# General path into the Else of one branch, other PSUM tiles for the splits, and POOL's weight residues in quarters: attention and mixture-of-experts kernel on one Trainium2 core

## Chip, cores and metric

The kernel runs on one core of a Trainium2 chip. The metric is the device time of one execution in microseconds (us): before the change a median of 1216.23 over 3 runs (1215.79 to 1216.82). PE is TensorE, DVE VectorE, ACT ScalarE, POOL GpSimd, SP SyncE.

## What is computed

An attention whose score maps are mixed over the 12 heads before and after the softmax, and a mixture of 8 experts on its rows, of which each row goes to one. All is fp32.

```python
B, H, S, D = 8, 12, 448, 64
s = einsum('bhij,hg->bgij', q @ k.T / sqrt(64), w_pre)
p = exp(s - s.max(-1)); p = p / (p.sum(-1) + 1e-9)
x = (einsum('bgij,gh->bhij', p, w_post) @ v)      # laid out as 3584 rows of 768
logits = x @ w_gate                               # 8 experts
e = logits.argmax(1); g = softmax(logits)[e]
out[row] = g * (relu(x[row] @ w1[e]) @ w2[e])     # w1: 768 x 1024, w2: 1024 x 768
```

## The kernel before

**Attention, to some 690 us.** The queries are worked off in tiles (`T`), and each tile in smaller steps: score matmuls (L275), a matmul that mixes heads (L308), reduce and exponentials (L314, L322), the inverse of the sums (`recip`, L330 and L332, operations on 124x2 elements in SBUF), the weights of the second mixing on POOL (L339), its matmuls (L355), and the product with v (L395, L417). The order of all this on every engine is written out by hand. At the end of each tile the rows of x go to DRAM, the expert of each row is chosen on VectorE (`choose`, `mark`), PE counts the rows of each expert by matmuls with the one-hot rows `ohb` (`rank`, L503), and `place` turns the counts into positions. `token`, `number` and `scatter` (L541 to L556) write the token's number and gate into the expert's list `TB` in DRAM.

**Getting expert 0 ready, beside the end of the attention.** A product of fp32 values is made from parts: a rounded value and its residue, three products instead of one. For expert 0's `w1`, six panels of 128x1024, the rounded part is ScalarE's (`round_w`), and the residue (raw less rounded) comes from `rest_w` (L583): panels 0 to 2 on POOL, between its L339 operations, and 3 to 5 on VectorE. The rows of expert 0 come in four slots of 128, gathered by indirect DMA. `turn` (L617) transposes a slot on PE into two PSUM tiles (part 0 is columns 0 to 255 of 768, part 1 the other 512), for slots 2 and 3 with rows of the last tile added by another matmul (L631). `split_x` (L633) rounds a part on ScalarE (L639) and takes the residue on VectorE (L640). Slot 0 uses the two banks of PSUM tile bs_106, slots 1 and 2 those of bs_107, slot 3 the tiles bm_108 and bm_109.

**The branches.** A number `flags` is computed from the counts (L911 to L918): bit e says that expert e has over 384 rows, the bits above the eighth that some expert has over 512. Only in the latter case is `beyond` needed, the general path: a loop over extra slots, each with its own gathers, weights, matmuls and stores. It has PSUM and SBUF pools of its own. Then the experts follow: `hidden(e, n)` is the first layer for n rows (8 x 6 x 3 = 144 matmuls at L1141, into four PSUM tiles pm_h, the first on the bank of bs_106 that slot 0's part 1 had), `result` the second layer for a slot (L1164). `hidden` exists in two copies, for 384 and 512 rows, behind a branch (L1186), and slot 3's `result` behind another (L1197).

With the data of these runs expert 0 has no more than 384 rows, and the general path isn't taken.

```python
with tc.If((flags >> NE) > 0):            # L1039
    beyond()
...
for e in range(NE):
    begin(e)
    long = (flags >> e) & 1
    widths = (CAP, SHORT) if e else (SHORT, CAP)          # 512 and 384
    with tc.If(long > 0 if e else long < 1) as cmp:       # L1186
        hidden(e, widths[0])
    with cmp.Else():
        hidden(e, widths[1])
```

Of the kernel before, what the change touches and what calls it, by code (L numbers as in the profile page):

```python
# [8 lines left out]
F32 = mybir.dt.float32  # L9
# [5 lines left out]
AF = mybir.ActivationFunctionType  # L15
ALU = mybir.AluOpType
AX = mybir.AxisListType
PSUM = bass.MemoryType.PSUM
# [3 lines left out]
HD = H * D  # L22
NT = B * S
NE, FF = 8, 1024
P = 128
# [9 lines left out]
CAP = 512  # L35
# [10 lines left out]
def attn_moe_kernel(ctx, tc, qT, kT, v, w_pre, w_post, w_gate, w1, w2, out):  # L46
# [536 lines left out]
    def rest_w(kt, engine):  # L583
        hi, lo = W["a", 0, kt]
        engine.tensor_sub(out=lo, in0=RAW.pop(("a", 0, kt)), in1=hi.bitcast(F32))
# [78 lines left out]
    side, side2 = ([bank[:, n, :] for n in (1, 0)] for bank in bank_s)  # L664
# [202 lines left out]
    turn(0, side)  # L867
# [9 lines left out]
    turn(1, side2)  # L877
# [7 lines left out]
    split_x(0, side)  # L885
    evict_x(T, 0)
    av(T, (1,), bank_m[1:])
    split_x(1, side2, (0,))
    evict_x(T, 1)
    split_x(1, side2, (1,))  # L890
# [9 lines left out]
    token(T - 1)  # L900
    number(T - 1)
    scatter(T - 1)
    gate(T)
    place(T)
    turn(2, side2, T)
# [18 lines left out]
    split_x(2, side2)  # L924
    rest_w(5, nc.vector)
    turn(3, bank_m, T)
    split_x(3, bank_m)
# [12 lines left out]
    def beyond():  # L940
# [11 lines left out]
        nc.vector.tensor_copy(out=total, in_=cum[:, NE - 1:NE])  # L952
        nslots = nc.values_load(total[0:1, 0:1], min_val=0, max_val=NT // P,
                                skip_runtime_bounds_check_because="a count of tokens over P")
        with tc.For_i(0, nslots, 1):
# [37 lines left out]
            xs = rt([P, HD], "oxs")  # L993
# [4 lines left out]
            u1 = rt([P, NK1, FF], "u1")  # L998
            u2 = rt([P, NK2, HD], "u2")
            for n, (u, w, nk) in enumerate(((u1, w1, NK1), (u2, w2, NK2))):  # L1000
                flat = w.rearrange("e r c -> (e r) c")
                for kt in range(nk):
                    nc.gpsimd.indirect_dma_start(
                        out=u[:, kt, :], out_offset=None, in_=flat,
                        in_offset=bass.IndirectOffsetOnAxis(ap=wi[:, n, kt:kt + 1], axis=0),
                        bounds_check=flat.shape[0] - 1, oob_is_err=False)
            xT = rt([P, NK1, P], "oxT")
            for kt in range(NK1):
                px = rest_ps.tile([P, 512], F32, name="opx")
                nc.tensor.transpose(out=px[:, :P], in_=xs[:, kt * P:(kt + 1) * P], identity=ident)  # L1010
                nc.vector.tensor_copy(out=xT[:, kt, :], in_=px[:, :P])
            hT = rt([P, NK2, P], "ohT")
            for ft in range(NK2):
                ph = rest_ps.tile([P, 512], F32, name="oph")
                for kt in range(NK1):
                    nc.tensor.matmul(out=ph[:, :P], lhsT=u1[:, kt, ft * P:(ft + 1) * P],
                                     rhs=xT[:, kt, :], start=(kt == 0), stop=(kt == NK1 - 1))
                nc.scalar.activation(out=hT[:, ft, :], in_=ph[:, :P], func=AF.Relu)
            yo = rt([P, HD], "oy")
            for g in range(2):  # L1020
                gs = slice(g * 384, (g + 1) * 384)
                py = rest_ps.tile([P, 512], F32, name="opy")
                for kt in range(NK2):
                    nc.tensor.matmul(out=py[:, :384], lhsT=hT[:, kt, :], rhs=u2[:, kt, gs],
                                     start=(kt == 0), stop=(kt == NK2 - 1))
                nc.vector.tensor_scalar(out=yo[:, gs], in0=py[:, :384], scalar1=tb[:, 1:2],
                                        scalar2=None, op0=ALU.mult)
# [4 lines left out]
    with ExitStack() as more:  # L1032
        rest = more.enter_context(tc.tile_pool(name="rest", bufs=1))
        rest_ps = more.enter_context(tc.tile_pool(name="rest_ps", bufs=1, space=PSUM))

        def rt(shape, name, dt=F32):
            return rest.tile(shape, dt, name=name)

        with tc.If((flags >> NE) > 0):  # L1039
            beyond()  # L1040
# [139 lines left out]
    for e in range(NE):  # L1180
        HH[e] = tuple(h_p.tile([P, NK2, CAP], F32R, name=f"h{x}") for x in "hl")
        begin(e)
        asked, order = dict(RAW), list(RAWS)
        long = (flags >> e) & 1
        widths = (CAP, SHORT) if e else (SHORT, CAP)
        with tc.If(long > 0 if e else long < 1) as cmp:  # L1186
            hidden(e, widths[0])
        RAW.clear()
        RAW.update(asked)
        RAWS[:] = order  # L1190
        with cmp.Else():
            hidden(e, widths[1])
# [38 lines left out]
```

## Time and profile before

| | us | share of the span |
|---|---|---|
| median of 3 runs | 1216.23 | |
| the profiled execution | 1215.08 | |
| its span | 1213.4 | |
| PE busy | 1183.0 | 97% |
| weight loads of PE busy | 992.4 | 82% |
| VectorE busy | 798.5 | 66% |
| ScalarE busy | 724.6 | 60% |
| POOL busy | 392.7 | 32% |

The profile is of one execution. Its time is 1.15 us under the median of the runs, and 1.7 us of it lie around the span. [...] Times of rows are in us from the start of the span. A timeline row gives start, duration, engine, line, operation, output and inputs, and in brackets how long the engine stood idle before and what ended that. PEld are the weight loads of PE, and an engine's name with q is its sequencer (branches, semaphores).

### The profile page before, as it was taken

The numbers are of one execution on the slowest core, as the hardware profiler recorded it, in microseconds if no ns is written. First come the engines' busy times: TensorE is split into PE (matmuls) and PEld (weight loads), VectorE is DVE, ScalarE is ACT, GpSimd is POOL, SyncE is SP. The second block draws the span as 40 slices with busy tenths as digits, with TensorE's granted clock in tenths as the row PEclk, the third lists the DMA queues.
The fourth block names the chain that finished last, engine by engine and source line by source line (L and its number), as shares of the span: only waits on it lengthen the run. The fifth ranks groups of instructions, "written<-read, shape, count | busy, mean of one in ns | idle before, by whom it ended". The sixth has DMA issues, their size and how long they took to land. (4 is left out here: it accounts for less than half of the span.)

```text
span 1213.4 us, 46361 instructions
## 1 busy us (share of the span) xinstructions
PE 1183.0 (97%) x19435; PEld 992.4 (82%) x19437; DVE 798.5 (66%) x1988; ACT 724.6 (60%) x1491; POOL 392.7 (32%) x613
## 2 busy tenths in 40 slices
PE   7999999999999999999999999999999999999996
PEld 3677787777777777877777799898989899989886
DVE  5887888878878878888788845444535344544320
ACT  5877777878777868778776545343434344444220
POOL 4443453544534535435344412020202002110100
PEclk9999999999999999999999999999999999999998
DMA  6666657566656566575656487465655647575300
GB/s 190 206 188 190 195 160 219 173 182 201 197 168 204 175 202 197 162 218 188 177 175 191 134 239 223 140 204 159 188 155 148 167 133 218 164 227 131 119 18 34
DMA packets 178793, 211.19 MB, mean 174 GB/s; under 512 B 85573, under 2 KB 156245, under 8 KB 178568
## 3 DMA queue, kind: packets, MB, share of 16 engines
q1 hardware_dynamic: 172504, 184.14, 52.0%
q0 software_dynamic: 6064, 23.86, 5.7%
q8 instruction: 164, 2.69, 1.0%
q14 instruction: 61, 0.50, 0.2%
HBM read 97.59 MB, written 23.07 MB: 99 GB/s over the span
## 5 line engine op out<-in xcount | busy, mean ns | idle before, releaser
L322 ACT ACTIVATE et<-bm,st 124x448 f32<-124x448 f32 x360 | 225.4, 631 | 156.6 <-DVE st L314 130.9
L314 DVE TENSOR_REDUCE st<-bm 124x1 f32<-124x448 f32 x360 | 208.4, 619 | 73.7 <-PE bm L308 67.0
L355 PEld LDWEIGHTS bp<-wp,et 64*64 64x64 f32 (+1 forms) x10052 | 196.5, 135 | 71.2 <-issue 49.1
L1141 PE MATMUL pm_h<-si,ah 128*128 128x512 f32 (+1 forms) x768 | 230.2, 381 | 3.1 <-DVE si L640 2.0
L373 DVE COPY pt<-bp 128x480 f32<-128x480 f32 x350 | 212.1, 648 | 2.4 <-PE bp L355 1.8
L339 POOL TENSOR_SCALAR wp<-Wpost,st 124x60 f32<-124x60 f32 x360 | 151.6, 436 | 170.0 <-DVE st L332 135.4
L355 PE MATMUL bp<-wp,et 64*64 64x60 f32 (+1 forms) x10052 | 190.4, 218 | 1.2 <-issue 1.1
L308 PE MATMUL bm<-sb,Wquad 60*60 60x448 f32 (+3 forms) x1408 | 185.1, 560 | 5.3 <-ACT et L322 3.5
L1141 PEld LDWEIGHTS pm_h<-si,ah 128*128 128x128 f32 x768 | 142.6, 188 | 29.8 <-issue 4.2
L285 ACT COPY si<-bs 120x896 f32<-120x896 f32 (+1 forms) x189 | 161.5, 910 | 3.8 <-PE bs L275 2.1
L1141 PE MATMUL pm_h<-si,al 128*128 128x512 f32 (+1 forms) x384 | 146.1, 380 | 0.0
L1145 DVE SCALAR_TENSOR_TENSOR hl<-pm_h,hh 128x512 fp32r<-128x512 f32 (+1 forms) x64 | 42.1, 658 | 140.8 <-ACT hh L1144 140.8
L417 PE MATMUL bs<-pt,vt 128*64 128x120 f32 (+1 forms) x2400 | 127.4, 261 | 1.2 <-ACT et L322 0.8
L1164 PE MATMUL pm_y<-bh,hl 128*128 128x384 f32 x480 | 121.8, 334 | 0.0
L1164 PE MATMUL pm_y<-bh,hh 128*128 128x384 f32 x480 | 121.8, 334 | 0.0
L1164 PE MATMUL pm_y<-bl,hh 128*128 128x384 f32 x480 | 121.8, 334 | 0.0
L1144 ACT ACTIVATE hh<-pm_h 128x512 fp32r<-128x512 f32 (+1 forms) x64 | 36.5, 571 | 141.3 <-PE pm_h L1141 141.3
L151 POOL TENSOR_TENSOR ql<-qr,qh 128x360 fp32r<-128x360 f32 (+1 forms) x78 | 69.8, 906 | 156.5 <-ACT qh L150 120.8
L656 POOL DMA_INDIRECT si<-XD,tcl x28 | 39.7, 1417 | 247.9 <-DVE y L1169 234.7
L417 PEld LDWEIGHTS bs<-pt,vt 128*64 128x64 f32 x2400 | 114.9, 137 | 5.7 <-issue 1.0
L1173 POOL DMA_INDIRECT out<-y,ti x30 | 31.1, 1038 | 187.4 <-ACT y L1171 71.6
L1164 PEld LDWEIGHTS pm_y<-bh,hh 128*128 128x128 f32 x480 | 86.8, 188 | 0.5
(172 smaller groups left out, 1731.7 us busy)
## 6 DMA issues: line engine op xcount, KB each, us to landing
sb<-si SPq DMA_DIRECT2D x344, 210.0 KB
wraw<-in_w SPq DMA_DIRECT2D x48, 512.0 KB
wraw<-in_w SPq DMA_DIRECT2D x64, 384.0 KB
vt<-in_v SPq DMA_DIRECT2D x64, 192.0 KB
kr<-in_kT SPq DMA_DIRECT2D x42, 224.0 KB
XD<-xr SPq DMA_DIRECT2D x48, 180.0 KB
qr<-in_qT SPq DMA_DIRECT2D x46, 180.0 KB
sb<-si SPq DMA_DIRECT2D x16, 189.0 KB
```

Of the source, the lines that this page charges most:

```text
L151: engine.tensor_sub(out=lo, in0=src, in1=hi.bitcast(F32))
L285: copy(out=SI[T][:ni, 2 * c:2 * c + 2, :], in_=bank[:ni, :, :S])
L308: nc.tensor.matmul(out=bank_m[r][CUT[c], :S], lhsT=Wquad[CUT[r], CUT[c]], rhs=sb[CUT[r], c, :], start=True, stop=True)
L314: nc.vector.reduce_max(out=st[:R1, 0, c:c + 1], in_=bank_m[c][:R1, :S], axis=AX.X, negate=True)
L322: nc.scalar.activation(out=et[:R1, c, :], in_=bank_m[c][:R1, :S], func=AF.Exp, bias=st[:R1, 0, c:c + 1], scale=1.0, accum_out=st[:R1, 1, c ...
L339: nc.gpsimd.tensor_scalar(out=wp[:R1, c, :H * IQ], in0=Wpost[:R1], scalar1=st[:R1, 2, c:c + 1], scalar2=None, op0=ALU.mult)
L355: nc.tensor.matmul(out=banks[r][col * JC:(col + 1) * JC, at_:at_ + W], lhsT=et[CUT[r], n, kg * JC:(kg + 1) * JC], rhs=wp[CUT[r], n, :W], s ...
L373: copy(out=flat[:, :, i0 + r * IB:i0 + (r + 1) * IB] .rearrange("p x (n k) -> p x n k", k=IQ), in_=banks[r][:, :2 * NJ * W].rearrange("p ( ...
L417: nc.tensor.matmul(out=HOME[T, g][r * D:(r + 1) * D, p, :], lhsT=VV[b][:, c, h * D:(h + 1) * D], rhs=PT[T][:, c, h, :ni], start=(c == 0), ...
L1141: nc.tensor.matmul(out=ph[:, :n], lhsT=wx[:, fs], rhs=xx, start=(m == 0), stop=(m == 3 * NK1 - 1))
L1145: nc.vector.scalar_tensor_tensor(out=hl[:, ft, :n], in0=ph[:, :n], scalar=0.0, in1=hh[:, ft, :n].bitcast(F32), op0=ALU.max, op1=ALU.subtract)
L1164: nc.tensor.matmul(out=py[g][:, :384], lhsT=hx[:, kt, ts], rhs=wx[:, g * 384:(g + 1) * 384], start=(n == 0), stop=(n == 3 * NK2 - 1))
```

## The change

There are four parts to it.

1. `rest_w` on POOL goes in four pieces of 256 columns; on VectorE it stays whole.
2. `homes` gives the slots other PSUM tiles: slot 0 bs_106 as before, slot 1 one bank of bs_107 and bp_111, slot 2 the other bank of bs_107 and bm_109, slot 3 bank 0 of bs_106 and bm_108.
3. `token`, `number` and `scatter` of the last but one tile move from behind `evict_r(T, 1)` to between the two parts of slot 0's split.
4. `beyond` is no longer called ahead of the experts. One branch asks whether the general path is not needed and expert 0 is short. If so, it runs the short `hidden` of expert 0; all else is in its Else: the general path (behind a branch of its own, followed by a second fetch of four `w2` panels), and expert 0's short and long `hidden`. The general path uses the experts' storage (hx, tx, RAWS, the pools y and pm_y) and streams the weights in panels.

```diff
     def rest_w(kt, engine):
-        hi, lo = W["a", 0, kt]
-        engine.tensor_sub(out=lo, in0=RAW.pop(("a", 0, kt)), in1=hi.bitcast(F32))
+        raw, (hi, lo) = RAW.pop(("a", 0, kt)), W["a", 0, kt]
+        width = FF // 4 if engine is nc.gpsimd else FF
+        for c in range(0, FF, width):
+            cs = slice(c, c + width)
+            engine.tensor_sub(out=lo[:, cs], in0=raw[:, cs], in1=hi[:, cs].bitcast(F32))
...
-    side, side2 = ([bank[:, n, :] for n in (1, 0)] for bank in bank_s)
+    homes = ([bank_s[0][:, 1, :], bank_s[0][:, 0, :]], [bank_s[1][:, 1, :], bank_p[1]],
+             [bank_s[1][:, 0, :], bank_m[1]], [bank_s[0][:, 0, :], bank_m[0]])
...
-    split_x(0, side)
+    split_x(0, homes[0], (0,))
+    token(T - 1)
+    number(T - 1)
+    scatter(T - 1)
+    split_x(0, homes[0], (1,))
...
     evict_r(T, 1)
-    token(T - 1)
-    number(T - 1)
-    scatter(T - 1)
     gate(T)
     place(T)
-    turn(2, side2, T)
+    turn(2, homes[2], T)
...
-    split_x(2, side2)
+    split_x(2, homes[2])
     rest_w(5, nc.vector)
-    turn(3, bank_m, T)
-    split_x(3, bank_m)
+    turn(3, homes[3], T)
+    split_x(3, homes[3])
...
-        with tc.If((flags >> NE) > 0):
-            beyond()
...
+        if e == 0:
+            with tc.If((flags & (((1 << NE + 4) - (1 << NE)) | 1)) < 1) as usual:
+                hidden(e, SHORT)
+            again()
+            with usual.Else():
+                with tc.If((flags >> NE) > 0):
+                    beyond()
+                    for kt in range(AHEAD_W):
+                        nc.sync.dma_start(out=RAW["b", e, kt], in_=w2[e, kt * P:(kt + 1) * P, :])
+                with tc.If(long < 1) as cmp:
+                    hidden(e, SHORT)
+                again()
+                with cmp.Else():
+                    hidden(e, CAP)
+        else:
+            with tc.If(long > 0) as cmp:
+                hidden(e, CAP)
...
```

What this makes of the order on the engines, at the places that the prediction speaks of:

ScalarE at the end of the attention phase, before: it reads the flags (`many`) and rounds the parts of slots 2 and 3, with what each waits for.

```order
L918 TENSOR_LOAD many [waits DVE_49]
L639 CAST si<-bs_107 128x2x128 [waits PE_49]
L639 CAST si<-bs_107 128x4x128 [waits DVE_49]
L639 CAST si<-bm_108 128x2x128 [waits PE_49]
L639 CAST si<-bm_109 128x4x128 [waits PE_49]
```

And now:

```order
L923 TENSOR_LOAD many [waits DVE_49]
L642 CAST si<-bs_107 128x2x128 [waits PE_49]
L642 CAST si<-bm_109 128x4x128 [waits PE_49]
L642 CAST si<-bs_106 128x2x128 [waits DVE_49,PE_49]
L642 CAST si<-bm_108 128x4x128 [waits PE_49]
```

The second cast of slot 2 waits for PE in the place of VectorE; slot 3's first part is now in bs_106.

PE before, from the end of the general path to expert 0's first matmuls (`ah` and `al` are a panel's two parts, the loop's branches are L955):

```order
L1024 MATMUL opy<-u_14366,ohT 128x384 x16
L955 REGISTER_ALU
L955 COMPARE_AND_BRANCH
L955 UNCONDITIONAL_BRANCH
L1039 UNCONDITIONAL_BRANCH
L1186 REGISTER_ALU
L1186 COMPARE_AND_BRANCH
L1141 MATMUL pm_h<-si,ah_13364 128x384 x2
```

PE now, at the end of the usual case's first layer and the beginning of what is jumped over:

```order
L1201 UNCONDITIONAL_BRANCH
L1205 REGISTER_ALU
L1205 COMPARE_AND_BRANCH
L963 TENSOR_LOAD total
L965 COMPARE_AND_BRANCH
L965 UNCONDITIONAL_BRANCH x2
L1254 BRANCH_PREFETCH_HINT
L1018 MATMUL pm_y<-ident,hx_14304 128x128 x6
```

The general path stood ahead of expert 0's first layer; it stands behind the usual copy of that layer, inside what the jump at L1201 passes over.

## Rows read from the trace of the kernel before

**Rows 1.** Stretches: window, length, busy of PE PEld DVE ACT POOL, clock, DMA, GB/s.

```profile
655.00:682.00 27.00, 24.29 (x702) 19.44 (x694) 24.11 (x74) 15.99 (x41) 17.67 (x23) 1.00 0.74 205
682.00:699.20 17.20, 14.40 (x220) 12.98 (x211) 13.59 (x55) 8.77 (x21) 4.43 (x5) 1.00 0.30 86
...
699.20:1202.30 503.10, 502.04 (x2592) 461.93 (x2592) 224.97 (x299) 200.79 (x255) 69.84 (x57) 1.00 0.55 160
```

**Rows 2.** Waits of PE: line, releaser, total us, times, longest us.

```profile
PE pm_h L1141 <- DVE si L640: 2.0, 1, 2.0
...
PE bs L503 <- DVE sc L495: 1.2, 1, 1.2
```

**Rows 3.** Timeline of 667.5 to 674 us, all engines.

```profile
667.56 2.35 POOL L585 TENSOR_TENSOR al<-wraw,ah 128x1024 fp32r<-128x1024 f32 x1
...
668.01 0.98 PE L308 MATMUL bm<-sb,Wquad 64*64 64x448 f32 x8
...
668.11 1.82 DVE L330 TENSOR_SCALAR st<-st 124x2 f32<-124x2 f32 x1
...
670.06 1.15 DVE L314 TENSOR_REDUCE st<-bm 124x1 f32<-124x448 f32 x2
...
673.40 0.22 PE L503 MATMUL bs<-ohb,tri 120*120 120x8 bf16 x1 [1.25 <-DVE sc L495]
```

**Rows 4.** Lines L330, L124 (ns min/median/max, first, last start); timeline, one step earlier.

```profile
L330 DVE TENSOR_SCALAR st<-st x184: 142/157/1825, 25.5 to 681.0; 124x2 f32<-124x2 f32 x176, 124x1 f32<-124x1 f32 x8
...
L124 POOL TENSOR_TENSOR kl<-kr,kh x42: 1130/1152/1183, 49.2 to 580.4; 128x448 fp32r<-128x448 f32 x42
...
661.50 0.98 PE L308 MATMUL bm<-sb,Wquad 64*64 64x448 f32 x8
...
662.62 0.62 DVE L314 TENSOR_REDUCE st<-bm 124x1 f32<-124x448 f32 x1 [0.39 <-PE bm L308]
```

**Rows 5.** Timeline of the attention phase's end, 683.9 to 699.2 us.

```profile
683.97 0.17 PE L503 MATMUL bs<-ohb,tri 120*120 120x8 bf16 x1 [0.45 <-DVE ohb L493]
...
687.93 0.69 DVE L640 TENSOR_TENSOR si<-bs,si 128x512 fp32r<-128x512 f32 x1 [0.65 <-ACT si L639]
...
694.45 0.15 DVE L543 TENSOR_SCALAR sc<-sc 88x1 f32<-88x1 f32 x1 [0.79 <-DVE many L917]
...
695.90 0.41 DVE L640 TENSOR_TENSOR si<-bs,si 128x256 fp32r<-128x256 f32 x1
696.35 0.59 ACT L639 CAST si<-bs 128x512 fp32r<-128x512 f32 x1 [1.50 <-DVE si L640]
...
696.97 0.69 DVE L640 TENSOR_TENSOR si<-bs,si 128x512 fp32r<-128x512 f32 x1 [0.65 <-ACT si L639]
...
697.58 1.23 DVE L585 TENSOR_TENSOR al<-wraw,ah 128x1024 fp32r<-128x1024 f32 x1
698.72 1.01 DVE L640 TENSOR_TENSOR si<-bm,si 128x256 fp32r<-128x256 f32 x2
```

**Rows 6.** Line L1039 on PE's sequencer, and the timeline at the first layer's start.

```profile
L1039 PEldq COMPARE_BRANCH  x1: 3565/3565/3565, 695.0 to 695.0; - x1
...
699.22 0.41 PE L1141 MATMUL pm_h<-si,ah 128*128 128x384 f32 x1 [2.03 <-DVE si L640]
```

**Rows 7.** Lines L1186 (all, and 720 to 724) and L1164; timeline at 724.

```profile
L1186 PEldq COMPARE_BRANCH  x15: 67/297/1224, 699.0 to 1164.8; - x15
...
L1186 PEldq COMPARE_BRANCH  x1: 325/325/325, 721.3 to 721.3; - x1
...
L1164 PEldq EVENT_SEMAPHORE  x5: 51/51/51, 721.7 to 722.1; - x5
...
724.28 0.36 PEld L1164 LDWEIGHTS pm_y<-bh,hh 128*128 128x128 f32 x2
```

**Rows 8.** Timeline at the change from expert 0 to expert 1.

```profile
746.44 1.03 DVE L1085 TENSOR_TENSOR si<-hx,si 128x256 fp32r<-128x256 f32 x2 [0.96 <-ACT si L1083]
...
750.12 0.72 PE L1141 MATMUL pm_h<-si,ah 128*128 128x512 f32 x2 [0.52 <-PEq L1197]
```

More of the change, by code (lines that the diff above doesn't have):

```diff
@@ L866, in attn_moe_kernel @@
     post(*final, banks=bank_m)
-    turn(0, side)
+    turn(0, homes[0])
     rank(T - 1)
@@ L876, in attn_moe_kernel @@
     round_w(5)
-    turn(1, side2)
+    turn(1, homes[1])
     for g in range(2):
@@ L884, in attn_moe_kernel @@
         gather(2 + n, ti2[:, n:n + 1], T - 1)
-    split_x(0, side)
+    split_x(0, homes[0], (0,))
[3 more added lines that the diff above has]
+    split_x(0, homes[0], (1,))
     evict_x(T, 0)
     av(T, (1,), bank_m[1:])
-    split_x(1, side2, (0,))
+    split_x(1, homes[1], (0,))
     evict_x(T, 1)
-    split_x(1, side2, (1,))
+    split_x(1, homes[1], (1,))
     logits(T, 0)
@@ L952, in beyond, with hT @@
         nc.vector.tensor_copy(out=total, in_=cum[:, NE - 1:NE])
+        xs, xT = hx[0], hx[1].rearrange("p (k x) -> p k x", x=P)
+        def hT(ft):
+            return tx[ft // 6][:, ft % 6 * P:(ft % 6 + 1) * P]
         nslots = nc.values_load(total[0:1, 0:1], min_val=0, max_val=NT // P,
@@ L992, in beyond @@
                                     op0=ALU.min, op1=ALU.add)
-            xs = rt([P, HD], "oxs")
             nc.gpsimd.indirect_dma_start(
@@ L997, in beyond @@
                 bounds_check=NT, oob_is_err=False)
[L998 to L1006, printed above, removed]
@@ L1007, in beyond, with chunk @@
-            xT = rt([P, NK1, P], "oxT")
+            def chunk(n, kt):
+                w, width = ((w1, FF), (w2, HD))[n]
+                flat, u = w.rearrange("e r c -> (e r) c"), RAWS[kt % 4][:, :width]
+                nc.gpsimd.indirect_dma_start(
+                    out=u, out_offset=None, in_=flat,
+                    in_offset=bass.IndirectOffsetOnAxis(ap=wi[:, n, kt:kt + 1], axis=0),
+                    bounds_check=flat.shape[0] - 1, oob_is_err=False)
+                return u
             for kt in range(NK1):
-                px = rest_ps.tile([P, 512], F32, name="opx")
+                px = pm_y.tile([P, 512], F32, name="pm_y")
@@ L1010, in beyond @@
                 nc.tensor.transpose(out=px[:, :P], in_=xs[:, kt * P:(kt + 1) * P], identity=ident)
                 nc.vector.tensor_copy(out=xT[:, kt, :], in_=px[:, :P])
-            hT = rt([P, NK2, P], "ohT")
-            for ft in range(NK2):
[L1014 to L1018, printed above, removed]
@@ L1019, in beyond @@
-            yo = rt([P, HD], "oy")
-            for g in range(2):
+            ph = [pm_y.tile([P, 512], F32, name="pm_y") for _ in range(2)]
+            for kt in range(NK1):
+                u = chunk(0, kt)
+                for ft in range(NK2):
+                    nc.tensor.matmul(out=ph[ft // 4][:, ft % 4 * P:(ft % 4 + 1) * P],
+                                     lhsT=u[:, ft * P:(ft + 1) * P], rhs=xT[:, kt, :],
+                                     start=(kt == 0 and ft % 4 == 0),
+                                     stop=(kt == NK1 - 1 and ft % 4 == 3))
@@ new lines, in beyond @@
+            for ft in range(NK2):
+                nc.scalar.activation(out=hT(ft), in_=ph[ft // 4][:, ft % 4 * P:(ft % 4 + 1) * P],
+                                     func=AF.Relu)
+            py2 = [pm_y.tile([P, 512], F32, name="pm_y") for _ in range(2)]
+            for kt in range(NK2):
+                u = chunk(1, kt)
+                for g in range(2):
+                    nc.tensor.matmul(out=py2[g][:, :384], lhsT=hT(kt), rhs=u[:, g * 384:(g + 1) * 384],
+                                     start=(kt == 0), stop=(kt == NK2 - 1))
@@ L1021, in beyond @@
+            yo = y_p.tile([P, HD], F32, name="y")
+            for g, py in enumerate(py2):
                 gs = slice(g * 384, (g + 1) * 384)
[L1022 to L1025, printed above, removed]
                 nc.vector.tensor_scalar(out=yo[:, gs], in0=py[:, :384], scalar1=tb[:, 1:2],
@@ L1030, in beyond, with rt @@
                 in_=yo, in_offset=None, bounds_check=NT - 1, oob_is_err=False)
[L1032 to L1037, printed above, removed]
-        with tc.If((flags >> NE) > 0):
-            beyond()
+    rest = moe.enter_context(tc.tile_pool(name="rest", bufs=1))
+    def rt(shape, name, dt=F32):
+        return rest.tile(shape, dt, name=name)
     wpool["b"] = moe.enter_context(tc.tile_pool(name="wb", bufs=1))
@@ L1184, in attn_moe_kernel, with again @@
         long = (flags >> e) & 1
[L1185 to L1192, printed above, removed]
+        def again():
+            RAW.clear()
+            RAW.update(asked)
+            RAWS[:] = order
+        if e == 0:
[15 more added lines that the diff above has]
+                hidden(e, CAP)
+            again()
+            with cmp.Else():
+                hidden(e, SHORT)
         for s in range(NS - 1):
```

## The prediction

> **What bounds the kernel now.** I read the stretches first: the columns are the window, its length, the busy time of PE, PEld, DVE, ACT and POOL, the granted clock, and the DMA share. [...] In the end of the attention phase PE is busy 24.29 of 27.00 us (655 to 682) and 14.40 of 17.20 (682 to 699.2) [rows 1], so 5.5 us are open there. The waits of PE show the largest hole, 2.0 us in front of the first matmul of L1141 [rows 2]. The timeline shows another, 1.25 us in front of L503 at 673.40 [rows 3]. The change touches what stands ahead of both.
>
> **The hole at 673.40.** POOL starts the residue of a weight panel at 667.56 and needs 2.35 us. The VectorE instruction of L330 issued at 668.11 takes 1.82 us and ends at 669.93, where POOL's ends (669.91) [rows 3]. The same instruction has a median of 157 ns over 184 [rows 4]: it was held for some 1.66 us. Behind it stand L314 (670.06), two evictions and the choice of the experts, for whose one-hot rows PE waits 1.25 us until 673.40 [rows 3].
>
> The change cuts this POOL operation into four of 256 columns. The trace has 1152 ns for 448 columns [rows 4] and 2.35 us for 1024, so 2.09 ns a column, and a quarter should take 1152 - 192 x 2.09 = 751 ns: 3.0 us for four, 0.65 more than now. The first quarter ends at 668.31. If L330 gets in there, it is done by 668.5, and the next limit is PE: L314 began 1.12 us after its L308 in the step before (661.50 and 662.62) [rows 4]. L308 starts at 668.01 [rows 3], so L314 can start at 669.13 instead of 670.06. That is 0.93 us earlier for all that follows, of PE's 1.25 us. Bounds: 1.25 us gained (the whole hole), and 0.65 us lost, if VectorE gets in only after the fourth quarter at 670.56. No row shows two POOL operations back to back with VectorE waiting, so this is open; I take **-0.93**, because the held L330 ended 0.02 us behind a single POOL instruction, so it is instructions that it waits for, and there are now four ends in the place of one.
>
> POOL's 0.65 us more, three times, I cost at nothing: the operation of four that comes last ends ahead of the weights for the last post matmuls, and behind those PE still stands idle for 0.45 us at 683.97, waiting for VectorE [rows 5]. If that reserve were gone, 0.2 us (0.65 - 0.45) would show.
>
> **The hole at 699.2: the VectorE side.** In the last stretch VectorE runs the residue of panel 4, slot 2's two parts (695.90 and 696.97), the residue of panel 5 (697.58) and slot 3's two parts (from 698.72) [rows 5]. Between the parts of slot 2 it stands idle for 0.65 us, waiting for ScalarE's cast at 696.35, which in turn had been idle for 1.50 us waiting for VectorE [rows 5]: both parts lie in one PSUM tile, and the second cast waits for VectorE to be done with the first part. The order of ScalarE shows that this wait goes, since part 1 now lies in another tile and waits for PE alone, whose transposes are ahead of the first part's cast too. So the second part can follow the first at once, and slot 3's first part ends 0.65 us earlier. It ends now at about 699.13 (698.72 + 0.41, the length of slot 2's first part), and will end at 698.48.
>
> The three small operations of token and number (0.15 us one, L543) move from behind mark to the 0.65 us for which VectorE stands idle in front of slot 0's second part (687.93) [rows 5], and I count them as nothing on either side. The scatter of the last but one tile leaves POOL earlier, and with it the last scatter, expert 0's list and the loads behind it on SP; none of these is waited for by PE, which stands idle for 1.06 us in all of the experts' 503 [rows 1], so nothing for this either.
>
> **The PE side.** PE's sequencer meets the branch around the general path at 695.0 and is held for 3565 ns, to 698.5; a second branch and the wait of L1141 follow, and the first matmul starts at 699.22 [rows 6]. The profile puts the 2.03 us down to L640; by its own rows the branch had ended only 0.7 us before, so it was as late as VectorE was. After the change the usual case runs straight on: one branch that falls through, and L1186 has branches of 67 ns [rows 7], so PE is there by 695.2. But the first accumulator is the first PSUM bank, which slot 3's first part now uses, so the first matmul has to wait for VectorE at 698.48. Start: 698.57 instead of 699.22, **-0.65**. Bounds: 0 (the branch is as slow as before), and 1.6 (a start right behind slot 2).
>
> **The new jump.** What is saved at the branch comes back behind expert 0's first layer. There PE has to jump over everything that the usual case doesn't run. Now it skips one copy of hidden (144 matmuls and 144 loads); this jump took 325 ns at 721.3 [rows 7]. Then it skips two copies and the whole general path. The same line's jumps have taken 67 to 1224 ns, and the only one over other code, at L1039, 3565 [rows 6, 7]. I take 3565, since a longer jump is nearer to the slowest than to the usual one: 3.24 us more. It is partly covered: the sequencer runs ahead of PE, its last semaphore row before L1164 ends at 722.2, and the first weight load of L1164 runs at 724.28 [rows 7], so 2.08 us are hidden, and **+1.16** are seen as a gap of PE. Bounds: 0 (a jump of up to 2.4 us is hidden) and 3.24 (no cover).
>
> [...]
>
> VectorE, ScalarE and SP make the same jump. If each lost as much, VectorE would be late by some 2 us in preparing expert 1; its last operation on the gathered rows ends at 747.5 and PE asks for them at 750.12 [rows 8], 2.6 us later. So nothing, unless the stall is longer than that.
>
> **The sum.** -0.93 - 0.65 + 1.16 = -0.42 us. The profiled execution took 1215.08 us (1213.4 of span and 1.7 around it), which makes 1214.66; the median of the runs is 1.15 above it, so the forecast is 1215.8.
>
> **The rivals.**
> - *The jump stays hidden.* For it: the median of PE's 15 branches at L1186 is 297 ns [rows 7], and 2.08 us are covered. Against it: 3565 ns at L1039. Time: -0.93 - 0.65 = -1.58, 1214.65. Chance 0.20.
> - *VectorE doesn't get in between the quarters.* [...] Then +0.65 stands for -0.93: +1.16, 1217.4. Chance 0.12.
> - *The gain at 673.40 is not passed on*, because another wait (a list or a row store by DMA) sets the end of the attention phase: -0.65 + 1.16 = +0.5, 1216.7. Chance 0.10.
> - *Slower: the jump costs two fetches.* If PE lands near the end of what was fetched, it waits again: 2 x 3.24 - 2.08 = 4.4 us at one place, at 724. With -1.58 this is +2.8, 1219.1. It decides from 4.0 us on. For it: one slow branch is on record; against it: PE's 1.06 us of gaps in 503 [rows 1]. Chance 0.06.
>
> **How the numbers follow.** The forecast has 0.48, the rivals 0.48 together, and 0.04 is left for a start still earlier than I see. A measurement of this kernel can tell about 0.2%, 2.4 us, from no change. All cases but the last lie within that. Faster by more: the remaining 0.04 and some of the first rival, if the whole 1.25 us come too, 0.08. Slower by more: the last rival and a little of the second, 0.08. The same: 0.84. The range takes in the first two rivals and the spread of the runs: 1213.9 to 1218.0.
>
> **What would show it.** Right: L330 near 668 takes under 0.9 us; PE's wait before L503 falls to some 0.3; no idle between VectorE's two parts of slot 2; PE waits for slot 3's first part before the first layer; a gap of about 1 us at PE's change to the second layer of expert 0, and in the other experts none above the 0.52 of 750.12 [rows 8]. Wrong: L330 still ends with the last POOL quarter; no gap at that change; or a new wait of PE in expert 1.

## The result, and the profile after

The changed kernel takes a median of **1228.84 us** (1227.77 to 1232.18, 6 runs) against 1216.01 before (1213.73 to 1220.0, 6 runs): a ratio of 1.0098, 95% interval 1.0073 to 1.0124, or 8.9 to 15.1 us more. The forecast was 1215.8, with a range from 1213.9 to 1218.0.

The profiled execution has a span of 1227.2 us, 13.8 more than the one before. The stretches, with the columns of [rows 1]:

```profile
655.00:682.00 27.00, 23.55 (x643) 18.31 (x636) 22.13 (x71) 15.09 (x39) 18.43 (x30) 1.00 0.72 205
682.00:700.08 18.08, 16.22 (x271) 14.66 (x271) 14.82 (x61) 9.65 (x23) 5.38 (x6) 1.00 0.29 82
700.08:725.77 25.69, 25.68 (x144) 25.36 (x144) 12.26 (x19) 12.00 (x17) 4.37 (x4) 1.00 0.82 259
725.00:730.00 5.00, 1.77 (x8) 1.47 (x7) 1.59 (x2) 1.01 (x2) 0.00 (x0) 0.86 1.18 229
730.00:735.30 5.30, 2.88 (x10) 2.69 (x10) 3.00 (x5) 3.02 (x4) 0.00 (x0) 0.50 0.51 44
735.30:740.00 4.70, 4.70 (x28) 4.70 (x27) 2.61 (x4) 2.87 (x3) 0.00 (x0) 0.98 0.83 165
700.08:1216.21 516.13, 509.43 (x2592) 468.98 (x2592) 225.41 (x300) 200.80 (x255) 68.46 (x57) 0.99 0.53 156
```

The last row runs from the first matmul of the first layer to the last matmul, 516.13 us. The same work took 503.17 before (699.22 to 1202.39), so **12.96 of the 13.8 us lie there**, and 0.86 ahead of it. (Another 0.5 us lies outside the span: 2.1 to 2.3 us around it in all six executions, 1.7 in the one before. Of the kernels below, the five others with the usual case in the If and the general path inside its Else have 1.9 to 2.4 too, all the rest 1.7 to 1.8; why is open.) Of the 12.96, PE stands idle for 5.66 more (516.13 - 509.43 = 6.70, against 1.04). The rest is work that got longer, in part at a granted clock of 0.50, half speed, from 730 to 735.3.

The waits of PE, and PE's timeline behind expert 0's first layer:

```profile
PE pm_y L1173 <- issue: 5.7, 2, 3.2
...
PE bp L355 <- issue: 3.3, 6, 1.5
...
PE pm_h L1150 <- DVE si L643: 1.3, 1, 1.3
```

```profile
729.00 0.98 PE L1173 MATMUL pm_y<-bh,hh 128*128 128x384 f32 x2 [3.23 <-issue]
729.77 0.52 PE L1173 MATMUL pm_y<-bl,hh 128*128 128x384 f32 x1
732.72 0.48 PE L1173 MATMUL pm_y<-bl,hh 128*128 128x384 f32 x1 [2.42 <-issue]
```

There are two gaps, 3.23 and 2.42 us, with three matmuls and four weight loads between them. The jump in front of the first one, in the view of line L1201 on PE's sequencer (the shorter of the two rows' branches is the one into the usual case):

```profile
L1201 PEldq COMPARE_BRANCH  x2: 103/3062/6022, 696.5 to 722.6; - x2
```

And what no view of before had hinted at, the second layer itself (page, part 5; the first row before, the second after):

```profile
L1164 PE MATMUL pm_y<-bl,hh 128*128 128x384 f32 x480 | 121.8, 334 | 0.0
```

```profile
L1173 PE MATMUL pm_y<-bh,hl 128*128 128x384 f32 x480 | 124.4, 340 | 0.0
```

The same 128x384 matmuls start 176.7 ns apart where they started 173.3 apart, in every expert: a layer of 192 takes 34.08 us in the place of 33.45. The first layers of 512 columns have not changed (233.3 ns).

At the end of the attention phase VectorE's L330 at 668.33 ends behind POOL's third quarter and not its fourth, and PE no longer waits ahead of L503, where [rows 3] had 1.25:

```profile
666.42 2.77 POOL L588 TENSOR_TENSOR al<-wraw,ah 128x256 fp32r<-128x256 f32 x4
...
668.33 0.21 DVE L330 TENSOR_SCALAR st<-st 124x2 f32<-124x2 f32 x1
...
672.71 0.22 PE L503 MATMUL bs<-ohb,tri 120*120 120x8 bf16 x1
...
675.80 0.40 PE L355 MATMUL bp<-wp,et 60*64 60x60 f32 x12 [1.50 <-issue]
```

But 3 us later PE waits 1.50 us for instructions (a 16 KB packet of the instruction queue q8 runs from 673.08 to 674.24, PE goes on at 675.80), and the gain is gone.

### The profile page after: what moved, and what is told of

Same layout as the page of the kernel before. It is cut to its first block, busy times and chain, and to the rows that moved or that the text cites. A ratio compares the mean times of both kernels' runs of the same rounds, so it can differ in the third digit from the quotient of the medians.

```text
span 1227.2 us, 46362 instructions
## 1 busy us (share of the span) xinstructions
PE 1191.1 (97%) x19435; PEld 999.6 (81%) x19437; DVE 798.2 (65%) x1988; ACT 724.2 (59%) x1491; POOL 392.2 (32%) x622
## 5 line engine op out<-in xcount | busy, mean ns | idle before, releaser
L322 ACT ACTIVATE et<-bm,st 124x448 f32<-124x448 f32 x360 | 225.1, 630 | 156.8 <-DVE st L314 131.3
L1173 PE MATMUL pm_y<-bh,hh 128*128 128x384 f32 x480 | 124.7, 341 | 3.2 <-issue 3.2
L1173 PE MATMUL pm_y<-bl,hh 128*128 128x384 f32 x480 | 124.6, 340 | 2.4 <-issue 2.4
L1173 PE MATMUL pm_y<-bh,hl 128*128 128x384 f32 x480 | 124.4, 340 | 0.0
```

What stands on the lines that cost most here:

```text
L322: nc.scalar.activation(out=et[:R1, c, :], in_=bank_m[c][:R1, :S], func=AF.Exp, bias=st[:R1, 0, c:c + 1], scale=1.0, accum_out=st[:R1, 1, c ...
L1173: nc.tensor.matmul(out=py[g][:, :384], lhsT=hx[:, kt, ts], rhs=wx[:, g * 384:(g + 1) * 384], start=(n == 0), stop=(n == 3 * NK2 - 1))
```

## The experiments

**How they are compared.** A kernel's executions scatter by some 4 us either way here, and chips differ (before: medians of 1216.1 to 1221.4 in the five sets below), so each median stands beside that of before in its own set. The sharper measure is in the profiles: from the first matmul of the first layer to the last matmul, "the experts" below, 503.17 us before. But each profile is of one execution: for pad, before_352, shift, early_shift, only_token and parts_kc it was the fastest of all, 1.8 to 6.8 us under the median, so a profile need not hold what the median lost.

| kernel | median, before's | ratio, 95% | experts | gaps behind the first layer |
|---|---|---|---|---|
| the change | 1228.8, 1216.0 | 1.0073 to 1.0124 | 516.13 | 3.23 + 2.42 |
| before_off | 1216.0, 1216.1 | 0.9979 to 1.0016 | 506.41 | none |
| pad | 1226.8, 1216.1 | 1.0069 to 1.0142 | 515.77 | 2.95 + 2.76 |
| turn_pad | 1222.5, 1216.1 | 1.0027 to 1.0073 | 509.51 | none |
| last | 1222.2, 1216.1 | 1.0036 to 1.0074 | 507.44 | none |
| behind | 1228.9, 1217.5 | 1.0055 to 1.0114 | 511.42 | 2.35 + 2.75 |
| before_352 | 1225.5, 1217.5 | 1.0036 to 1.0082 | 508.06 | none |
| parts | 1222.3, 1217.5 | 1.0009 to 1.0053 | 503.02 | none |
| behind_turn | 1222.5, 1217.5 | 1.0013 to 1.0053 | 504.04 | none |
| before_again | 1221.5, 1221.4 | 0.9977 to 1.0021 | 504.70 | none |
| shift | 1228.3, 1221.4 | 1.0035 to 1.0082 | 508.08 | 2.83 |
| early | 1229.8, 1221.4 | 1.0049 to 1.0108 | 509.75 | 2.53 + 2.15 |
| early_shift | 1227.6, 1221.4 | 1.0038 to 1.0082 | 505.94 | 2.24 |
| only_rest | 1219.0, 1219.3 | 0.9970 to 1.0014 | 505.63 | none |
| only_homes | 1219.8, 1219.3 | 0.9978 to 1.0021 | 504.69 | none |
| only_token | 1220.1, 1219.3 | 0.9995 to 1.0030 | 503.21 | none |
| before_kc | 1218.4, 1219.3 | 0.9972 to 1.0010 | 503.21 | none |
| no_path | 1222.4, 1217.6 | 1.0016 to 1.0053 | 505.71 | 2.49 |
| parts_kc | 1221.1, 1217.6 | 1.0003 to 1.0040 | 502.96 | none |

### Set 1: the address, and the place of the jump

The build's table of tiles puts bh0, the first of the second layer's 16 panels, at byte 98752 before and at 99104 after: the general path's small tiles, 352 bytes, were freed ahead of it and now stay. The first guess was alignment.

```diff
+    moe.enter_context(tc.tile_pool(name="fill", bufs=1)).tile([P, 8], F32, name="fill")
     wpool["b"] = moe.enter_context(tc.tile_pool(name="wb", bufs=1))
```

> The kernel before, with one unused tile of 32 bytes a partition ahead of the second layer's weight panels, so that bh and bl start 32 bytes off a multiple of 64, as they do in the changed kernel (which never used such a tile: its general path's small tiles stay allocated there). Nothing else differs. Theory (the place of the moving panels costs 3.3 ns a matmul of the second layer): a second layer of 192 matmuls takes 34.08 us in the place of 33.45, one of 144 matmuls 25.6 in the place of 25.15; in all 1344 + 144 matmuls of L1164, so 1216.0 + some 4.7 = 1220.7. Rival (the slower second layer is due to the other PSUM banks, or to this chip's run): 33.45 us as before, 1216.

The second layers of the first six experts ran at 173.3 ns a matmul (33.44 us for 192), those of the last two at 176.6 (34.08), in one execution, with one code and one set of addresses; the median didn't move. An offset of 32 bytes is not the rule.

```profile
853.84:887.20 33.36, 33.36 (x192) 33.12 (x191) 1.00 0.62 186
1173.18:1207.20 34.02, 34.02 (x192) 33.75 (x191) 1.00 0.09 35
```

(Windows of PE and its weight loads, line L1165, two second layers.) The slow one had less DMA traffic beside it, so traffic isn't it either.

```diff
     rest = moe.enter_context(tc.tile_pool(name="rest", bufs=1))
+    rest.tile([P, 8], F32, name="fill")
```

> The changed kernel with one more unused tile of 32 bytes in the pool of the general path, so that bh and bl start at a multiple of 64 bytes again. Theory of the place: a second layer falls from 34.08 to 33.45 us, in all 4.7 us: 1228.8 - 4.7 = 1224.1; the two gaps of PE behind expert 0's first layer (3.23 and 2.42 us) stay. Rival (PSUM banks): nothing, 1228.8.

33.95 us a layer, 176.0 ns a matmul: a third cadence, at byte 99136. The guess falls a second time, and the two gaps stay.

```diff
-            with tc.If((flags & (((1 << NE + 4) - (1 << NE)) | 1)) < 1) as usual:
-                hidden(e, SHORT)
-            again()
-            with usual.Else():
+            with tc.If((flags & (((1 << NE + 4) - (1 << NE)) | 1)) > 0) as rare:
...
+            again()
+            with rare.Else():
+                hidden(e, SHORT)
```

> As pad, and the one branch turned round: the rare case in the If, the usual first layer of expert 0 in its Else. PE now jumps over the rare case ahead of the first layer and runs straight on behind it. Theory (the gaps and the slow clock behind them come from the jump over code that has to be fetched): no gap of PE behind expert 0's first layer, clock 1.00 there, 5.65 + 2.2 us less than pad; the jump lies ahead of the first layer, where PE waits for VectorE until some 1.3 us after its last matmul in any case, so the hole there grows to what the jump takes, 3.6 to 6 us from 696.5: 0.3 to 2.7 us. In all 1224.1 - 7.9 + 0.3 to 2.7 = 1216.5 to 1218.9. Rival (the gaps belong to the second layer's own start, its weights or expert 0's row transposes by DMA): they stay, 1224 to 1227.

The gaps behind the first layer are gone, and with them 515.77 - 509.51 = 6.3 us: they belong to the jump. The hole ahead of the first layer grew to 2.12 us, as expected (pad has 1.34); that the clock falls behind it, to a mean of 0.78 from 697.4 to 705 us, was not expected.

```diff
...
+    with tc.If((flags >> NE) > 0):
+        beyond()
     manual.close()
     moe.close()
```

> The changed kernel with bh and bl at a multiple of 64 bytes and the general path called behind the last expert instead of inside expert 0's branch; expert 0's branch is that of the kernel before (two copies of the first layer). PE's jump over the general path then comes behind its last matmul, while VectorE, POOL and the stores are still busy for some 10 us. Theory: no gap behind expert 0's first layer, no jump ahead of it; left are the gains of the pieces on POOL (0.9 us) and of the other PSUM tiles (0.65): 1216.0 - 1.6 = 1214.4. Rival (the gain at POOL's pieces is lost again in the attention phase, as in the profile of the changed kernel): 1216 - 0.65 = 1215.4 or more.

No gap, but 1222.2: the addresses (33.95 us a layer, experts +4.3), and the general path's place at the end isn't free, as I had thought: from the last matmul to the end of the span it is 15.4 us (1203.57 to 1219.0), where before has 11.0. It isn't PE's jump, which takes 0.35 us there: POOL's last drain begins behind the branch, at 1210.31, and before had it begin 1.25 us behind the last matmul.

### Set 2: the same addresses, exchanged

```diff
-    rest = moe.enter_context(tc.tile_pool(name="rest", bufs=1))
...
     tx = [xg.rearrange("p c x -> p (c x)")[:, :HD], half_p.tile([P, HD], F32, name="tx")]
+    rest = moe.enter_context(tc.tile_pool(name="rest", bufs=1))
...
```

> The changed kernel with the pool of the general path's small tiles opened behind the others, so that bh, bl, y, hx and tx stand at the very addresses of the kernel before (bh from byte 98752 in the place of 99104). Nothing else differs. Theory (the cadence of the second layer's matmuls follows the address of the moving panels, though not in steps of 32 bytes): a second layer takes 33.45 us again (173.3 ns a matmul) in the place of 34.08 (176.7), 4.7 us in all: 1228.8 - 4.7 = 1224. Rival (the cadence is a phase that PE falls into at the start of a layer, whatever the addresses): 33.95 or 34.08 us stay, 1227 to 1229. The two gaps of PE behind expert 0's first layer stay in both.

```diff
+    moe.enter_context(tc.tile_pool(name="fill", bufs=1)).tile([P, 88], F32, name="fill")
     wpool["b"] = moe.enter_context(tc.tile_pool(name="wb", bufs=1))
```

> The counterpart: the kernel before with an unused tile of 352 bytes ahead of the second layer's panels, so that bh, bl, y, hx and tx stand at the addresses that they have in the changed kernel (bh from 99104). Theory of the address: second layers of 34.08 us (176.7 ns a matmul), 1216.1 + 4.7 = 1220.8. Rival (phase): 33.45 us in most layers, 1216.1, as with 32 bytes.

The windows of the experts and of expert 1's second layer in the changed kernel at before's addresses, and then in before at the changed kernel's:

```profile
704.92:1216.34 511.42, 505.16 (x2592) 464.33 (x2592) 225.49 (x300) 201.19 (x255) 68.43 (x57) 0.99 0.54 158
797.53:830.90 33.37, 33.37 (x194) 33.37 (x193) 17.53 (x25) 14.02 (x16) 8.88 (x7) 1.00 0.60 186
```

```profile
697.91:1205.97 508.06, 507.02 (x2592) 466.79 (x2592) 226.23 (x302) 200.78 (x255) 70.40 (x57) 1.00 0.54 159
782.97:817.00 34.03, 34.03 (x194) 34.03 (x193) 17.53 (x25) 14.00 (x16) 8.87 (x7) 1.00 0.58 176
```

Exchanged addresses exchange the cadence, in every second layer of both. **The address is worth 4.7 us** (516.13 - 511.42) in the one direction and 4.9 (508.06 - 503.17) in the other. In the second layers of experts 1 to 7 alone, where no gap and no slow clock enters, it is 4.1 and 4.2. The medians don't show it as clearly: behind is still 11.5 us over the before of its set, where 8 were expected and the change has 12.8, and before_352 is 8.0 over, where 4.7 were expected. The twelve kernels of sets 2 to 5 that follow, all at 98752, have 173.3. Which property of the address it is stays open, and by before_off it isn't the address alone.

The next is parts: the first three of the four parts of the change, whose diff stands ahead of the prediction, on the kernel before.

> The kernel before with the first three parts of the change alone: the residues on POOL in quarters, the other PSUM tiles for the splits, and token, number and scatter at their new place. Branches, general path and addresses are those of before. Theory (these parts gain 0.9 us at 673 and up to 0.65 at the first layer, where the branch around the general path now ends last): 1216.1 - 0.9 to 1.6 = 1214.5 to 1215.2, second layers of 33.45 us. Rival (phase: a first layer that starts at another moment brings another cadence): second layers of 33.95 or 34.08 us and up to 1220.

Experts 503.02, a hole of 0.96 us ahead of them, and yet a median of 1222.3 against 1217.5. The profiled execution took 1217.85, so it holds little of this loss. Its experts begin at 702.15, 4.2 us later than those of before_352 (697.91) on the same chip: what it shows of the loss sits ahead of the experts. Sets 4 and 5 go on with it.

> As behind, and the branch turned round, so that PE jumps ahead of expert 0's first layer and not behind it. Theory of the address: second layers of 33.45 us; no gap behind the first layer; a hole of some 2.1 us ahead of it, with 1.6 us for a clock that falls there, as in the run turned round with the other addresses: 1222.4 - 4.2 = 1218.2. Rival (phase): 33.95 us, 1222.4.

(Edit: the turned branch of turn_pad and the moved pool of behind, without pad's tile.) Experts 504.04. What is left over 503.17 lies in expert 0's first layer, mostly a gap in it:

```profile
711.98 0.52 PE L1150 MATMUL pm_h<-si,ah 128*128 128x384 f32 x2 [0.46 <-issue]
```

The clock is 1.00 there, behind a hole of 2.14 us. The median is 5.0 us over before all the same.

### Set 3: the two gaps

> The kernel before once more, unchanged, for a second profile of it beside the others of this set. Second layers of 33.45 us (173.3 ns a matmul) if that follows the addresses; first layer of the experts from about 699 us. On another chip the kernels profiled beside each other had stretches of PE between 672 and 700 us in which its instructions came in fours, 0.75 us apart, and a lower granted clock behind them, and began the first layer 2 to 8 us later: if that is a matter of the chip or the moment, it can be here too, and in all four; if it came with the change's first parts, it isn't here.

Second layers of 33.45 us again. PE was held 4645 ns by the branch at L1039, the hole ahead of the first layer was 3.11 us, the clock 0.50 behind it, and PE's instructions came in small groups near 679 and 694, behind gaps of 0.42 and 0.41 us and of 0.21 and 0.33 (all issue): that isn't the change's own.

```diff
             with usual.Else():
+                for _ in range(4):
+                    spare = pm_y.tile([P, 512], F32, name="pm_y")
+                    for n in range(4):
+                        nc.tensor.transpose(out=spare[:, n * P:(n + 1) * P], in_=ident, identity=ident)
```

> As behind (addresses of before), with 16 more transposes (16 matmuls and 16 weight loads) at the start of the code that the usual case jumps over; they never run. The target of PE's jump moves by 32 instructions, nothing else. Theory (the second gap, 2.4 us, is another wait for code: the target lies some 8 instructions ahead of the end of what one fetch brings, so that PE runs out again): the second gap goes, the first stays, 2.4 us less than behind, or a little more if the clock falls for less long. Rival (the second gap is the second layer's own, of its weights or of the clock): two gaps, as before.

The waits of PE in behind, and then in shift:

```profile
PE pm_y L1173 <- issue: 5.1, 2, 2.7
```

```profile
PE pm_y L1173 <- issue: 2.8, 1, 2.8
```

Code that never runs takes the second gap away, and 511.42 - 508.08 = 3.3 us with the clock behind it. So the second gap is a second wait for code, and the target's place decides it. The packets of the instruction queue q8 say the same: in the changed kernel one of 16 KB runs from 726.18 to 727.21 and PE goes on at 728.6, the next from 730.28 to 731.28 and PE goes on at 732.72. (In shift the profiled execution took 1222.04, the fastest of six; the median's distance from before, 6.8 us against 11.5 in behind, is on another chip.)

```diff
-            if e == 0 and ft == 4:
+            if e == 0 and ft == 2:
                 halves_x(0)
                 halves_x(1)
```

> As behind, with expert 0's row transposes by DMA (two on SP, in expert 0's first layer) asked behind the third piece of the layer and not the fifth, some 6 us earlier, so that they are over when PE jumps. Theory (PE's fetch of the code behind the jump waits in the DMA queues behind these transposes: it began 3.58, 3.15 and 2.77 us after the jump in three profiles, when the second of them ended, against 0.6 us at the branch of the kernel before): the fetch starts after some 0.6 us, the jump takes 3.0 to 3.6 us in the place of 5.1 to 6.0, and the first gap falls from 2.4 to 3.2 us to about 0.5 to 1.0; the clock doesn't fall behind it, or falls for less long: 2 to 4 us less than behind. Rival (the fetch is late for another reason): jump and gap stay.

SP's timeline, and line L1201 of that kernel:

```profile
718.30 2.45 SPq L1083 DMA_TRANSPOSE xg<-hx  x1
720.82 2.96 SPq L1083 DMA_TRANSPOSE tx<-hx  x1
723.88 3.74 SPq L573 DMA_DIRECT2D wraw<-in_w  x4
```

```profile
L1201 PEldq COMPARE_BRANCH  x2: 103/2692/5282, 703.1 to 728.2; - x2
```

The transposes were over at 723.8, the jump came at 728.2, and it still took 5282 ns: the theory of the transposes falls. Why this fetch begins 2.5 to 3.6 us after the jump, and the one at the old branch after 0.6 in the first profile, is open.

> Both of the last two. Theory: one gap of 0.5 to 1.0 us behind expert 0's first layer, no fall of the clock there, second layers of 33.45 us; that is before, less the gains of the first parts (0.9 and up to 0.7 us), plus this gap: 0 to 1 us under before. Rival: what is left of the difference between the changed kernel with the addresses of before (some 11 us over before on the chip where it ran) and the 7.5 us of the gaps and the clock stays, and it is 2 to 4 us over before.

One gap of 2.24 us, no fall of the clock behind it, experts 505.94. The median is 6.1 us over before, more than even the rival's 2 to 4; the experts explain 2.8 of it (1.2 against before_again on the same chip) and the time around the span 0.6. The profiled execution was only 2.5 over (1223.89).

### Sets 4 and 5: the first three parts, and how far a jump may go

Each part alone, on the kernel before: `rest_w` in quarters (only_rest), `homes` (only_homes), and the new place of `token`, `number` and `scatter` (only_token), as in the change's diff.

> The kernel before with the residues on POOL in quarters, and nothing else changed. Theory (VectorE gets in between the quarters, 0.9 us less of PE's wait at 673): 0.9 us less than before, within what the runs scatter. Rival (VectorE's earlier start of the step moves loads or PE's fetch of code against each other, and PE then runs short of instructions between 672 and 700 us more often than in before): 2 to 6 us more than before, with PE's instructions in fours, 0.75 us apart, in the profile.

> The kernel before with the other PSUM tiles for the four slots, and nothing else changed. Theory: slot 2's second part no longer waits for the first, up to 0.65 us less where VectorE sets the start of the first layer, nothing where the branch around the general path does: 0 to 0.65 us less than before. Rival (the three parts' loss of 4.8 us sits here): 2 to 6 us more.

> The kernel before with token, number and scatter of the last but one tile at their new place, and nothing else changed. Theory: no difference, within 0.2%. Rival (the earlier scatter brings the list and the weight loads behind it earlier, and these hold up PE's fetch of code): 2 to 6 us more than before.

-0.3, +0.5 and +0.8 us, each known to some 2 to 3 us either way: no part alone can be told from no change.

```diff
-    keep_clock(bank_p[0], 2)
+    keep_clock(bank_p[0], 8)
```

> The kernel before with eight idle matmuls in the place of two ahead of the branch (512 columns each, on the bank that they use now). PE works them off while its sequencer is held by the branch. Theory (where the hole ahead of the first layer is long, 2.6 and 3.1 us in two profiles of before's branch, the clock falls behind it and the first 9 matmuls or so take 0.32 us each, some 1.5 us; after 2.03 us it didn't): the hole shrinks by some 1.3 us, the clock stays 1.00, and the median is up to 1.5 us lower. Rival (the idle matmuls delay the first layer, or the clock falls for another reason): no difference or up to 1.3 us more.

The hole shrank to 1.47 us (2.87 and 2.89 in only_rest and only_homes beside it, with the clock falling there in both; but their branches held PE for 4.4 us and this one for 3.6, so not all of it need be the idle matmuls), the clock stayed at 1.00, experts 503.21. The median is 0.9 us lower, an interval that holds no change. It is the lowest against its own before, and shown to beat nothing.

```diff
...
             with usual.Else():
-                with tc.If((flags >> NE) > 0):
-                    beyond()
-                    for kt in range(AHEAD_W):
-                        nc.sync.dma_start(out=RAW["b", e, kt], in_=w2[e, kt * P:(kt + 1) * P, :])
                 with tc.If(long < 1) as cmp:
```

> As behind, with the general path (which these data don't need) and the second fetch of four panels left out of the Else, so that PE jumps over two copies of the first layer, some 580 instructions in the place of some 870. Theory (a jump over more than PE has at hand costs a fetch of 5 to 6 us in all, 2.8 of them hidden, however far it goes beyond that; the jump over one copy, some 290 instructions, has code at hand): the slow jump and the first gap of 2.2 to 3.2 us stay, a second gap only where the target lies near the end of what the fetch brings. Rival (the cost grows with the general path's length): a jump of some 0.3 us, no gap, 1 us around before.

```profile
L1203 PEldq COMPARE_BRANCH  x2: 103/2702/5302, 698.4 to 723.1; - x2
```

5302 ns without the general path, one gap of 2.49: a jump over two copies of the first layer (some 580 instructions) is slow too. One copy (some 290) takes 325 ns [rows 7], but not everywhere. In eight profiles one jump over a single copy, at a later expert, took 3.27 to 4.26 us; it stayed hidden there. In the changed kernel it is behind expert 4's first layer:

```profile
L1215 PEldq COMPARE_BRANCH  x1: 3879/3879/3879, 991.6 to 991.6; - x1
```

In shift and early_shift, whose code lies 32 instructions further on, the jump at that place took 0.39 us. So the place in the code counts as well as the distance. Jumps over 580 and some 870 instructions took 5.03 to 6.02 us in all seven profiles that have one behind expert 0's first layer; those over 290 were slow only at some places. Where the bound lies, and what sets it, no run shows.

> The first three parts together on the old branch, as in the run of the parts, with eight idle matmuls ahead of the branch in the place of two. Theory (the loss of 4.8 us that the three parts showed on one chip is not theirs, as each by itself showed none on another chip: it came with PE's shortage of instructions, which kernels with and without them have): 0 to 2 us under before. Rival (the three together lose what none loses alone): 3 to 5 us over before.

3.5 us over before (0.4 to 4.9), on another chip: the rival. The three parts together lose, though no one of them does measurably; their three medians add up to +1.0 us, and whether the parts need each other to lose, or small losses add up, isn't shown. What the profiles hold of the loss is ahead of the experts (502.96). From the 351st of the 360 exponentials (L322) to the last L503, the eight profiles with all three parts on the chips of sets 2 to 5 take 34.6 to 36.9 us, and the six with one or none 32.9 to 34.0. On the chip of set 1 it was 30.2 to 30.9 with the parts and 31.6 without, so there they didn't lose. The clock goes with it: between 670 us and the experts' start, other than at the hole ahead of them, it fell to 0.50 in seven of the eight (all but parts_kc), and in one of the six (only_token). The executions as a whole point the same way: the mean granted clock of parts' twelve is 0.9926, of the thirty of before beside them 0.9949. By an estimate from these two, 0.0023 x 1217, that is at most 2.8 of the 4.8 us. PE's timeline in the profile of parts, where PE stands still and the profile shows nothing that it waits for:

```profile
689.88 0.39 PE L417 MATMUL bm<-pt,vt 128*64 128x88 f32 x4 [0.35 <-issue]
690.62 0.46 PE L417 MATMUL bm<-pt,vt 128*64 128x88 f32 x6 [0.35 <-issue]
691.39 0.43 PE L417 MATMUL bm<-pt,vt 128*64 128x88 f32 x5 [0.31 <-issue]
```

## Why the prediction was wrong

**The new jump: right place, wrong size.** It forecast +1.16 us from a jump of 3565 ns. It took 6022 in the change and 5030 to 5742 in six more profiles; 2.7 to 2.8 us of each stayed hidden, where the forecast's terms hide 2.4 (325 ns and 2.08 us). So the first gap is 3.23; and there is a second fetch behind it, 2.42, which shift shows to hang on where the target lies. That was the slower rival, "the jump costs two fetches", priced at 4.4 us for the two and given 0.06; the two were 5.66. The 0.06 was so low because of "PE's 1.06 us of gaps in 503 [rows 1]", a stretch in which no jump as long as this one stands; for the size there was one row, "one slow branch is on record". Even that row was no constant: the branch around the general path ahead of the experts took 0.39 to 4.65 us in the nine later profiles that have it there.

**The clock behind the gaps was in no term.** The forecast priced gaps as idle time alone. Behind them the clock stood at 0.50 until 735.3. Expert 0's first 48 matmuls of the second layer took 4.4 us more than at 176.7 ns each; 2.4 of that is the second gap and **2.0 is the clock**. In [rows 1] the clock is 1.00 everywhere, and a gap of 2.03 us [rows 2] left it there. Ahead of the first layer, where PE had been working with pauses (in before_again busy for 4.46 of 5 us from 690, 4.85 of 5 from 695), it fell at gaps of 2.12, 2.58, 2.87, 2.89 and 3.11 us, but not at the one of 2.14 in behind_turn. Behind the first layer, where PE had been busy throughout (25.68 of 25.69 us), it held at single gaps of 2.24 and 2.49 us and fell at one of 2.83.

**The step that failed outright is that the sum has the experts' stretch grow by a gap of PE alone.** The stretch grew by 12.96 us, and gaps are 5.66 of it. The change moved 352 bytes of tiles and with them all that is allocated behind; PE's matmuls then start 176.7 ns apart. 6 x 192 + 2 x 144 = 1440 of them at 3.3 ns are 4.8 us; behind and before_352 measured 4.7 and 4.9. No term had it, because the diff shows no address. Gaps, clock and address together are some 12.5 of the 12.96.

**The hole at 699.2: right.** From the last L503 to the first layer it took 7.73 us before (691.49 to 699.22) and 7.05 after (693.03 to 700.08), 0.68 less, against a forecast of 0.65. The first matmul waits for slot 3's first part, as said, VectorE has no idle time between the two parts of slot 2, and PE's branch takes 103 ns.

**The hole at 673.40: the wait went, but mostly by luck, and there was no gain.** L330 took 0.21 us, and the four quarters 2.77 (forecast 3.0). But L330 was issued 1.91 us behind POOL's start (666.42 and 668.33), where before it was 0.55 (667.56 and 668.11): one whole operation of 2.35 us would have ended at 668.77, only some 0.2 us behind the third quarter. And a quarter's end doesn't always let VectorE in. In all thirteen profiles with quarters L330 was issued during the third; in ten it ended behind that one, in shift, behind_turn and only_rest behind the fourth, so the rival of 0.12 holds in three. From only_rest:

```profile
665.32 2.77 POOL L588 TENSOR_TENSOR al<-wraw,ah 128x256 fp32r<-128x256 f32 x4
...
666.84 1.28 DVE L330 TENSOR_SCALAR st<-st 124x2 f32<-124x2 f32 x1
```

The hole itself was an accident of the one profiled execution: in the other six profiles with whole residues PE waits at that L503 for 0.44 us at most. And the 0.93 us were lost at once to the wait of 1.50 at 675.80. The rival "not passed on" had this for 0.10, by another wait.

**The reserves** held: expert 1's first layer begins behind a gap of 0.52 us, as in [rows 8].

## What to carry to other kernels

A branch that lets the usual case run straight on only moves the jump to its end: count the instructions that are jumped there (580 and more took 5.03 to 6.02 us in all seven profiles with such a jump behind the first layer; 290 were slow at some places, 3.27 to 4.26), and put the jump where PE waits anyway, with enough queued work ahead of it to keep the clock (eight idle matmuls in before_kc, where it stayed at 1.00). Ahead of a change that moves or frees a pool, compare the build's addresses of everything allocated behind it: a shift of 352 bytes cost 4.7 us here, and the diff was meant to gain 1.6. And before a wait of one profile goes into a sum, look whether a second profile has it.

## What the runs showed that was not expected

- The second layers' matmuls of 384 columns start 173.3, 176.0 or 176.7 ns apart (expert 5's first layer has 173.3, 174.7 or 176.7), a steady pattern over a whole layer. In the second layers it follows the moving panels' address, but at byte 98784 one execution went from 173.3 to 176.7 behind a gap of 0.52 us.
- Sixteen transposes that are never run took the second gap away, 3.3 us of the profiled experts, by moving the target of a jump.
- PE's instructions came in fours to sixes, some 0.75 us apart, near 675 and 690 us, in the profiles of all fourteen kernels of sets 2 to 5 and in none of set 1. Near 690 the eight with all three parts have four gaps of some 0.3 us each, the six others one to four. What makes it so on those chips is open, and with it why the three parts together lose there.
